# Float64 weights to float32 on the chip: shifts, masks and an integer addition in place of mantissa times exponent

## The chip, the cores and the metric

The kernel runs on one core of a Trainium2 chip. The time is that of one execution on the device, in microseconds (us). A core has five engines with their own in-order queues: TensorE (PE in the profile, PEld for its weight loads), VectorE (DVE), ScalarE (ACT), GpSimd (POOL) and SyncE (SP), which here issues all the transfers.

## The reference

Three stages, each on 8 batches of 576 positions and 512 features:

```python
kv = np.einsum('bhsd,bhse->bhde', k, v)            # attention without softmax
out = np.einsum('bhsd,bhde->bhse', q, kv)
x = out / np.sqrt(np.mean(out * out, -1, keepdims=True) + 1e-06) * g_norm

mixed = np.real(np.fft.fft(np.fft.fft(x, axis=1), axis=2))    # stage 2 (after heads are joined)
u = x + mixed
un = (u - mean(u)) / np.sqrt(var(u) + 1e-06)
x = u + np.maximum(un @ w_ch1, 0.0) @ w_ch2                   # 512 x 2048 and 2048 x 512

u = x + (x.transpose(0, 2, 1) @ U @ V).transpose(0, 2, 1)     # stage 3, U and V of rank 32
return u + np.maximum(u @ w_ch1, 0.0) @ w_ch2                 # its own w_ch1, w_ch2
```

The four weight matrices and U, V come as float64, because they are scaled by a float64 number; everything else is float32.

## The kernel before, in words

The positions (8 x 576 = 4608) are cut into 9 blocks of 512. Each of the two multilayer stages runs over the 9 blocks, and a block over 16 iterations, one per 128 of the 2048 hidden features: 12 matmuls for the hidden layer (`emit_l1`, L162), 12 for the output (`emit_l2`, L177). Every factor is split into a high part and a rest (`w1h`, `w1l`, `w2h`, `w2l`, `gh`, `gl`, `xh`, `xl`), so that each product is three matmuls. Iteration n, in the loop at L779, emits the split of the second weights (`split_w2`: ScalarE copies the high part, VectorE or, in iterations 5 to 9 of the first block, GpSimd subtracts), the hidden matmuls with `gh` on ScalarE and `gl` on VectorE, the split of the first weights two iterations ahead (`split_w1`, the subtraction on GpSimd or in some iterations on VectorE), then the output matmuls of the iteration before and a list of side tasks. The order on every engine is the order in which the program writes the instructions down (`manual_schedule`, L676); the lists `side` (L664) say which task stands in which iteration. During stage 2 the side tasks prepare the attention and the Fourier transform of the next batch: sums of squares (L267), powers (L269), norms (L280, L282), foldings (L295 to L330), transforms (L349 to L384).

The conversion. A weight tile is 128 x 512 float64 words. `raw_load` (L74) brings them, as pairs of 32-bit words, into one of two buffers `raw`; a load is issued for the tile two further on when a tile is converted (`w_next`, L119). `convert` (L99) takes a pair of tiles: `conv_a` for both, then `conv_b` for both. `lw` and `hw` are the low and the high words, 8 bytes apart. Per tile:

- L85, VectorE: the exponent bits of the high word into `pw`. L86, ScalarE: eight times that with the bias 896 taken off, as a number, which gives the bits of the float32 power of two. L87, ScalarE: the low word as a float, times 2^-52.
- L88, VectorE: the mantissa bits with the leading one, into the tile itself. L93, VectorE: the sign into `pw`. L95, VectorE: mantissa times 2^-20 plus the low part. L97, GpSimd: that times `pw`.

`pw` (tag `cv1`) has two buffers. Tiles of stage 2 are converted by `w_conv` (L115): one pair before the loop in two halves (L719 to L728), one pair each at L734 and L745, and 13 pairs in iterations 0 to 12 of block 0 (L766). Tiles of stage 3 are converted in stage 2 by `w_pre` (L124), which writes the result to DRAM, in iterations 0, 7 and 9 (`PRE`) of blocks 1 to 5 and once in block 6. Three more conversions (U and V) follow in block 7 (`t_b_tables`, L539). In all these places the conversion stands at the end of the iteration's side tasks.

Of the kernel before, what the change touches and what calls it, by code (L numbers as in the profile page):

```python
# [10 lines left out]
F32 = mybir.dt.float32  # L11
F32R = mybir.dt.float32r
U32 = mybir.dt.uint32
AF = mybir.ActivationFunctionType
ALU = mybir.AluOpType
# [17 lines left out]
VPAD = 192  # L33
EPS = 1e-6


@with_exitstack
def kernel(ctx: ExitStack, tc: tile.TileContext, qT, kvm, kvt, gn, w1a, w2a, w1b, w2b,
                      ucat, v4, tabs, outT):
    nc = tc.nc  # L40
    f32 = lambda ap: ap.bitcast(F32)

    com = ctx.enter_context(tc.tile_pool(name="com", bufs=1))
# [23 lines left out]
    ident = com.tile([128, 128], F32, name="ident")  # L67
    xe0 = com.tile([C, 3, B], F32, name="xe0")
    nhalf = com.tile([128, 8], F32, name="nhalf")
    ebias = com.tile([128, 1], F32, name="ebias")  # L70
    muT = com.tile([128, NT // 128], F32, name="muT")


# [5 lines left out]

    def conv_a(raw, out):  # L80

        n = raw.shape[1]
        lw, hw = raw[:, :, 0], raw[:, :, 1]
        pw = com.tile([128, 512], U32, tag="cv1", name="cv1", bufs=2)[:, 0:n]
        nc.vector.tensor_scalar(out=pw, in0=hw, scalar1=0x7FF00000, scalar2=None, op0=ALU.bitwise_and)  # L85
        nc.scalar.activation(out=pw, in_=pw, func=AF.Relu, scale=8.0, bias=ebias)  # L86
        nc.scalar.activation(out=f32(lw), in_=lw, func=AF.Copy, scale=2.0 ** -52)  # L87
        nc.vector.tensor_scalar(out=out.bitcast(U32), in0=hw, scalar1=0xFFFFF, scalar2=0x100000,  # L88
                                op0=ALU.bitwise_and, op1=ALU.bitwise_or)
        return raw, out, pw  # L90

    def conv_b(raw, out, pw):
        nc.vector.scalar_tensor_tensor(out=pw, in0=raw[:, :, 1], scalar=0x80000000, in1=pw,  # L93
                                       op0=ALU.bitwise_and, op1=ALU.bitwise_or)
        nc.vector.scalar_tensor_tensor(out=out, in0=out.bitcast(U32), scalar=2.0 ** -20, in1=f32(raw[:, :, 0]),  # L95
                                       op0=ALU.mult, op1=ALU.add)
        nc.gpsimd.tensor_tensor(out=out, in0=out, in1=f32(pw), op=ALU.mult)  # L97

    def convert(*pairs):  # L99
        for c in [conv_a(*p) for p in pairs]:  # L100
            conv_b(*c)
# [298 lines left out]
    def load_kv(b):  # L400
        kv = at.tile([128, 2, 5, DM], F32, tag="slot_a", name=f"kv{b}")
        for c in (slice(0, 256), slice(256, 512)) if b == 0 else (slice(0, 512),):
            for a in range(2):
                nc.sync.dma_start(out=kv[:, a, 0:4, c], in_=kvm[b][:, a, :, c])
            nc.sync.dma_start(out=kv[0:64, :, 4, c], in_=kvt[b][:, :, c])
        st.setdefault(b, {})["kv"] = kv
# [269 lines left out]
    with tc.manual_schedule():  # L676
        make_identity(nc, ident)
        nc.vector.memset(nhalf, -0.5)
        nc.vector.memset(kvbd, 0.0)
        nc.vector.memset(ebias, -896.0 * 2.0 ** 23)  # L680
        load_kv(0)
        load_q(0)
        nc.sync.dma_start(out=gnb, in_=gn)
# [33 lines left out]
        load_kv(1)  # L717
        t_s1(0, 0, 0)
        cv = [conv_a(raws.pop(0), w_new(0))]  # L719
        t_s1(0, 0, 1)  # L720
        t_s1(0, 1, 0)
        t_s1(0, 1, 1)
        conv_b(*cv[0])
        t_s2(0, 0)
        cv.append(conv_a(raws.pop(1), w_new(1)))
        t_ln_first(0)
        conv_b(*cv[1])
        w_next((0, 1))  # L728
        done = 2
# [158 lines left out]
```

## Time and profile before

| | |
|---|---|
| median of 3 runs | 1957.66 us (1957.63 to 1962.66) |
| the profiled execution | 1957.75 us, its span 1956.0 us |
| TensorE busy | 1849.6 us (95% of the span) |
| VectorE busy | 1000.8 us (51%) |
| ScalarE busy | 780.0 us (40%) |
| GpSimd busy | 769.8 us (39%) |
| granted TensorE clock, mean | 0.976 |

The span runs from the first to the last instruction of the profiled execution; its own time is 1.75 us longer. A busy time is the time in which an engine has an instruction running, also one that is running but held up. A duration in a row includes what the instruction waits once it has started; the step from one start to the next on the same engine is what it costs when the engine is full.

### The profile page before, as it was taken

The numbers are of one execution on the slowest core, as the hardware profiler recorded it, in microseconds if no ns is written. First come the engines' busy times: TensorE is split into PE (matmuls) and PEld (weight loads), VectorE is DVE, ScalarE is ACT, GpSimd is POOL, SyncE is SP. The second block draws the span as 40 slices with busy tenths as digits, with TensorE's granted clock in tenths as the row PEclk, the third lists the DMA queues.
The fourth block names the chain that finished last, engine by engine and source line by source line (L and its number), as shares of the span: only waits on it lengthen the run. The fifth ranks groups of instructions, "written<-read, shape, count | busy, mean of one in ns | idle before, by whom it ended". The sixth has DMA issues, their size and how long they took to land.

```text
span 1956.0 us, 22839 instructions
## 1 busy us (share of the span) xinstructions
PE 1849.6 (95%) x8520; PEld 1516.8 (78%) x8520; DVE 1000.8 (51%) x1525; ACT 780.0 (40%) x1460; POOL 769.8 (39%) x592
## 2 busy tenths in 40 slices
PE   4667899999899998999999999999999999999999
PEld 3556678878787887878888888888888888888887
DVE  5898785776757576574443333333333333333232
ACT  4444344444434444343434343434343433333332
POOL 4486665554545554453322223232223222222322
PEclk7878999999999999999999999999999999999999
DMA  4524415133241422302303301010101010100000
GB/s 137 192 86 150 174 44 193 68 119 130 73 146 54 163 98 97 133 10 74 87 33 131 122 1 49 1 44 1 49 0 44 1 49 1 44 1 22 1 22 22
DMA packets 62545, 140.05 MB, mean 72 GB/s; under 512 B 11273, under 2 KB 13786, under 8 KB 59618
## 3 DMA queue, kind: packets, MB, share of 16 engines
q1 hardware_dynamic: 62434, 138.59, 20.7%
q8 instruction: 67, 1.10, 0.2%
q14 instruction: 44, 0.36, 0.1%
HBM read 100.78 MB, written 36.73 MB: 70 GB/s over the span
## 4 chain that ended last, share of the span: by engine, by line
PE 75%; DVE 12%; POOL 6%; issue 3%; DMA 2%; ACT 2%; SPq 0%; DVEq 0%; POOLq 0%; ACTq 0%
PE h L168 11%; PE h L170 11%; PE h L169 11%; PE acc L193 7%; PE acc L194 7%; PE acc L192 7%; PE acc L188 4%; PE acc L190 4%; PE acc L189 4%; POOL ss L269 2%; PE kv L244 2%; POOL x L282 2%; DMA raw<-in_w2a 2%; DVE f L301 2%; DVE eh L330 1%
## 5 line engine op out<-in xcount | busy, mean ns | idle before, releaser
L146 POOL TENSOR_TENSOR w1l<-w,w1h 128x512 fp32r<-128x512 f32 x274 | 357.3, 1304 | 976.6 <-ACT w1h L145 953.3
L174 DVE SCALAR_TENSOR_TENSOR gl<-h,gh 128x512 fp32r<-128x512 f32 x288 | 198.3, 689 | 393.5 <-ACT gh L173 393.4
L173 ACT ACTIVATE gh<-h 128x512 fp32r<-128x512 f32 x288 | 171.4, 595 | 502.8 <-PE h L170 502.7
L154 DVE TENSOR_TENSOR w2l<-w,w2h 128x512 fp32r<-128x512 f32 x283 | 208.9, 738 | 188.4 <-ACT w2h L153 187.6
L188 PE MATMUL acc<-w2h,gl 128*128 128x512 f32 x576 | 235.4, 409 | 46.0 <-DVE gl L174 45.9
L153 ACT ACTIVATE w2h<-w 128x512 fp32r<-128x512 f32 x288 | 180.8, 628 | 160.7 <-PE acc L194 113.0
L189 PE MATMUL acc<-w2l,gh 128*128 128x512 f32 x576 | 232.0, 403 | 7.3 <-POOL w2l L154 7.3
L168 PE MATMUL h<-xl,w1h 128*128 128x512 f32 x576 | 230.0, 399 | 2.9 <-ACT w1h L145 1.4
L190 PE MATMUL acc<-w2h,gh 128*128 128x512 f32 x576 | 231.6, 402 | 0.0
L168 PE MATMUL h<-xlb,w1h 128*128 128x512 f32 x576 | 231.1, 401 | 0.0
L170 PE MATMUL h<-xhb,w1l 128*128 128x512 f32 x576 | 228.3, 396 | 0.0
L170 PE MATMUL h<-xh,w1l 128*128 128x512 f32 x576 | 226.2, 393 | 2.2 <-POOL w1l L146 2.2
L169 PE MATMUL h<-xhb,w1h 128*128 128x512 f32 x576 | 228.1, 396 | 0.0
L169 PE MATMUL h<-xh,w1h 128*128 128x512 f32 x576 | 226.2, 393 | 0.0
L194 PE MATMUL acc<-gh,w2h 128*128 128x512 f32 x576 | 225.4, 391 | 0.0
L193 PE MATMUL acc<-gl,w2h 128*128 128x512 f32 x576 | 225.4, 391 | 0.0
L192 PE MATMUL acc<-gh,w2l 128*128 128x512 f32 x576 | 224.7, 390 | 0.0
L145 ACT ACTIVATE w1h<-w 128x512 fp32r<-128x512 f32 x288 | 179.3, 623 | 23.2 <-POOL w L97 23.2
L188 PEld LDWEIGHTS acc<-w2h,gl 128*128 128x128 f32 x576 | 111.5, 194 | 79.2 <-DVE gl L174 56.0
L189 PEld LDWEIGHTS acc<-w2l,gh 128*128 128x128 f32 x576 | 112.2, 195 | 31.3 <-POOL w2l L154 8.7
L190 PEld LDWEIGHTS acc<-w2h,gh 128*128 128x128 f32 x576 | 112.5, 195 | 24.5
L170 PEld LDWEIGHTS h<-xh,w1l 128*128 128x128 f32 x576 | 109.3, 190 | 26.3 <-POOL w1l L146 2.6
(164 smaller groups left out, 2845.4 us busy)
## 6 DMA issues: line engine op xcount, KB each, us to landing
kv<-in_kvm SPq DMA_DIRECT2D x14, 1024.0 KB, 6.5
q<-in_qT SPq DMA_DIRECT2D x8, 1220.0 KB
x_d<-x2o SPq DMA_DIRECT2D x36, 256.0 KB, 2.1
x2f<-x_d SPq DMA_DIRECT2D x36, 256.0 KB, 3.8
outT<-o SPq DMA_DIRECT2D x36, 256.0 KB, 2.0
raw<-in_w1a SPq DMA_DIRECT2D x16, 512.0 KB, 3.4
raw<-in_w2a SPq DMA_DIRECT2D x16, 512.0 KB, 3.7
u_d<-x SPq DMA_DIRECT2D x32, 256.0 KB, 2.6
```

The costliest lines, as they stand in the source:

```text
L146: (nc.vector if n in on_dve else nc.gpsimd).tensor_tensor(out=al, in0=a, in1=f32(ah), op=ALU.subtract)
L154: (nc.gpsimd if n in CLP else nc.vector).tensor_tensor(out=cl, in0=c, in1=f32(ch), op=ALU.subtract)
L168: nc.tensor.matmul(out=h, lhsT=ah[:, kc, :], rhs=xl[:, kc, :], start=(kc == 0), stop=False)
L169: nc.tensor.matmul(out=h, lhsT=ah[:, kc, :], rhs=xh[:, kc, :], start=False, stop=False)
L170: nc.tensor.matmul(out=h, lhsT=al[:, kc, :], rhs=xh[:, kc, :], start=False, stop=(kc == 3))
L174: nc.vector.scalar_tensor_tensor(out=gl, in0=h, scalar=0.0, in1=f32(gh), op0=ALU.max, op1=ALU.subtract)
L188: nc.tensor.matmul(out=a, lhsT=gl[:, tt], rhs=ch, start=s, stop=False)
L189: nc.tensor.matmul(out=a, lhsT=gh[:, tt], rhs=cl, start=False, stop=False)
L190: nc.tensor.matmul(out=a, lhsT=gh[:, tt], rhs=ch, start=False, stop=e)
L192: nc.tensor.matmul(out=a, lhsT=cl[:, tt], rhs=gh, start=s, stop=False)
L193: nc.tensor.matmul(out=a, lhsT=ch[:, tt], rhs=gl, start=False, stop=False)
L194: nc.tensor.matmul(out=a, lhsT=ch[:, tt], rhs=gh, start=False, stop=e)
```

## The change

`ebias` and its memset go, and the conversion of a tile becomes: ScalarE takes the absolute value of the high word, read as a float32; VectorE clamps it between two constants (the patterns 0x38000000 and 0x47EFFFFF); ScalarE multiplies the low word by 2^-29 and stores it as an integer, which leaves its upper three bits, rounded; VectorE shifts the clamped word left by three and masks it. Then VectorE puts the top two bits of the high word and the rounded low part together in `pw`, and GpSimd adds the two as 32-bit integers. The places of the conversion, the buffers and the loads stay. Per tile VectorE has three instructions where it had four, ScalarE two as before, GpSimd one as before; the first instruction of a tile is now on ScalarE.

```diff
+HMIN, HMAX = (float(v) for v in np.array([0x38000000, 0x47EFFFFF], np.uint32).view(np.float32))
...
-    ebias = com.tile([128, 1], F32, name="ebias")
...
         lw, hw = raw[:, :, 0], raw[:, :, 1]
         pw = com.tile([128, 512], U32, tag="cv1", name="cv1", bufs=2)[:, 0:n]
-        nc.vector.tensor_scalar(out=pw, in0=hw, scalar1=0x7FF00000, scalar2=None, op0=ALU.bitwise_and)
-        nc.scalar.activation(out=pw, in_=pw, func=AF.Relu, scale=8.0, bias=ebias)
-        nc.scalar.activation(out=f32(lw), in_=lw, func=AF.Copy, scale=2.0 ** -52)
-        nc.vector.tensor_scalar(out=out.bitcast(U32), in0=hw, scalar1=0xFFFFF, scalar2=0x100000,
-                                op0=ALU.bitwise_and, op1=ALU.bitwise_or)
+        nc.scalar.activation(out=f32(pw), in_=f32(hw), func=AF.Abs)
+        nc.vector.tensor_scalar(out=f32(pw), in0=f32(pw), scalar1=HMIN, scalar2=HMAX, op0=ALU.max, op1=ALU.min)
+        nc.scalar.activation(out=lw, in_=lw, func=AF.Copy, scale=2.0 ** -29)
+        nc.vector.tensor_scalar(out=out.bitcast(U32), in0=pw, scalar1=3, scalar2=0x3FFFFFF8,
+                                op0=ALU.logical_shift_left, op1=ALU.bitwise_and)
         return raw, out, pw
 
     def conv_b(raw, out, pw):
-        nc.vector.scalar_tensor_tensor(out=pw, in0=raw[:, :, 1], scalar=0x80000000, in1=pw,
+        nc.vector.scalar_tensor_tensor(out=pw, in0=raw[:, :, 1], scalar=0xC0000000, in1=raw[:, :, 0],
                                        op0=ALU.bitwise_and, op1=ALU.bitwise_or)
-        nc.vector.scalar_tensor_tensor(out=out, in0=out.bitcast(U32), scalar=2.0 ** -20, in1=f32(raw[:, :, 0]),
-                                       op0=ALU.mult, op1=ALU.add)
-        nc.gpsimd.tensor_tensor(out=out, in0=out, in1=f32(pw), op=ALU.mult)
+        nc.gpsimd.tensor_tensor(out=out.bitcast(U32), in0=out.bitcast(U32), in1=pw, op=ALU.add)
...
-        nc.vector.memset(ebias, -896.0 * 2.0 ** 23)
```

## Rows read from the trace of the kernel before

**Rows 1.** The page, the chain that ended last, share by engine.

```profile
PE 75%; DVE 12%; POOL 6%; issue 3%; DMA 2%; ACT 2%; SPq 0%; DVEq 0%; POOLq 0%; ACTq 0%
```

**Rows 2.** Busy times by stage; the first row names the columns.

```profile
core 0: us, PE busy (x) PEld busy (x) DVE busy (x) ACT busy (x) POOL busy (x), PEclk, DMA share, GB/s
...
93.00:246.00 153.00, 119.94 (x505) 93.93 (x505) 126.20 (x188) 69.54 (x132) 105.35 (x69) 0.88 0.41 136
246.00:361.00 115.00, 110.89 (x548) 92.41 (x547) 78.58 (x123) 49.27 (x99) 58.96 (x46) 0.99 0.32 111
361.00:476.00 115.00, 110.91 (x549) 92.45 (x547) 78.74 (x123) 49.38 (x99) 59.13 (x46) 0.99 0.32 111
...
945.00:1956.00 1011.00, 1007.13 (x4460) 820.39 (x4458) 342.82 (x505) 375.68 (x651) 271.18 (x211) 1.00 0.10 34
```

**Rows 3.** Groups, 79 to 246 us: count, busy us, mean ns, idle before and releasers.

```profile
L97 POOL TENSOR_TENSOR w<-w,cv 128x512 f32<-128x512 f32 x28 | 45.9, 1648 | 36.8 <-DVE w L95 36.8
L95 DVE SCALAR_TENSOR_TENSOR w<-w,raw 128x512 f32<-128x512 uint32 x28 | 28.3, 1012 | 0.0
L93 DVE SCALAR_TENSOR_TENSOR cv<-raw,cv 128x512 uint32<-128x512 uint32 x28 | 20.5, 733 | 3.8 <-ACT cv L86 3.8
L86 ACT ACTIVATE cv<-cv,ebias 128x512 uint32<-128x512 uint32 x28 | 20.1, 718 | 30.0 <-DVE cv L85 30.0
L87 ACT ACTIVATE raw<-raw 128x512 f32<-128x512 uint32 x28 | 18.8, 670 | 0.0
L85 DVE TENSOR_SCALAR cv<-raw 128x512 uint32<-128x512 uint32 x28 | 16.6, 592 | 9.0 <-DMA raw<-in_w1a 5.9 <-DMA raw<-in_w2a 2.0 <-POOL w L97 1.2
```

**Rows 4.** VectorE in order of time, iteration 0 of block 2: start us, us, instruction.

```profile
364.54 0.42 DVE L88 TENSOR_SCALAR wpre<-raw 128x512 uint32<-128x512 uint32 x1
364.88 0.42 DVE L85 TENSOR_SCALAR cv<-raw 128x512 uint32<-128x512 uint32 x1
...
365.55 0.69 DVE L93 SCALAR_TENSOR_TENSOR cv<-raw,cv 128x512 uint32<-128x512 uint32 x1
366.17 0.68 DVE L95 SCALAR_TENSOR_TENSOR wpre<-wpre,raw 128x512 f32<-128x512 uint32 x1
...
367.37 1.76 DVE L95 SCALAR_TENSOR_TENSOR wpre<-wpre,raw 128x512 f32<-128x512 uint32 x1
369.06 0.68 DVE L154 TENSOR_TENSOR w2l<-w,w2h 128x512 fp32r<-128x512 f32 x1
...
370.26 1.20 DVE L146 TENSOR_TENSOR w1l<-w,w1h 128x512 fp32r<-128x512 f32 x1
371.38 1.28 DVE L280 TENSOR_TENSOR x<-x,ss 128x512 f32<-128x512 f32 x2
```

**Rows 5.** GpSimd in order of time, the same stretch.

```profile
367.10 1.49 POOL L97 TENSOR_TENSOR wpre<-wpre,cv 128x512 f32<-128x512 f32 x1
369.21 1.69 POOL L97 TENSOR_TENSOR wpre<-wpre,cv 128x512 f32<-128x512 f32 x1 [0.63 <-DVE wpre L95]
```

**Rows 6.** ScalarE in order of time, the same stretch.

```profile
362.64 0.62 ACT L265 ACTIVATE x<-o 128x512 f32<-128x512 f32 x1
364.66 0.73 ACT L86 ACTIVATE cv<-cv,ebias 128x512 uint32<-128x512 uint32 x1 [1.40 <-DVE cv L85]
365.29 0.67 ACT L87 ACTIVATE raw<-raw 128x512 f32<-128x512 uint32 x1
```

**Rows 7.** VectorE in order of time, start-up.

```profile
54.77 0.86 DVE L85 TENSOR_SCALAR cv<-raw 128x512 uint32<-128x512 uint32 x1
...
57.03 0.69 DVE L95 SCALAR_TENSOR_TENSOR w<-w,raw 128x512 f32<-128x512 uint32 x1
...
64.26 0.43 DVE L85 TENSOR_SCALAR cv<-raw 128x512 uint32<-128x512 uint32 x1 [1.06 <-DMA raw<-in_w2a]
...
66.74 1.75 DVE L95 SCALAR_TENSOR_TENSOR w<-w,raw 128x512 f32<-128x512 uint32 x1
```

**Rows 8.** Who waited for whom, whole span: us in total, times, longest us.

```profile
ACT cv L86 <- DVE cv L85: 65.8, 43, 5.4
...
DVE cv L93 <- ACT cv L86: 4.7, 4, 2.6
```

**Rows 9.** Line 97: count, least, median and greatest ns, first and last start us.

```profile
L97 POOL TENSOR_TENSOR w<-w,cv x32: 1260/1645/2868, 52.4 to 225.8; 128x512 f32<-128x512 f32 x32
```

**Rows 10.** Groups of ScalarE, whole span, columns as in Rows 3.

```profile
L248 ACT ACT_TABLE_LOAD x1 | 1.3, 1283 | 1.5 <-DVE ebias L680 1.5
```

## The prediction, made before the changed kernel was timed

> **What bounds the kernel now.** I read the chain that ended last first, then the busy times by stage, the costliest groups of the first block, and last the engines' order of time at one place of each kind. The chain is TensorE for 75% of the span, VectorE for 12% and GpSimd for 6% [rows 1]: a shorter conversion can only touch the last two. The stages say where they lie [rows 2]. Blocks 1 and 2 take 115 us each with TensorE busy 110.9 of them, and from 945 us on it is busy 1007 of 1011. Block 0 takes 153 us for the same matmuls, with VectorE busy 126 and GpSimd 105. Its difference to block 1 is the conversion: 13 pairs of weight tiles in block 0, three pairs (iterations 0, 7 and 9) in each of blocks 1 to 5, one in block 6. So there are three places to price: the start-up up to 79 us, the 14 pairs from 79 to 246 us, and the pair at iteration 0 of blocks 1 to 6. Iterations 7 and 9 of those blocks lie where the chain is TensorE, and the three late conversions of U and V come after 945 us, where TensorE fills the time; a shorter conversion there I cost at nothing, covered by the matmuls. Without that cover the ten pairs would be worth 12 us more at the price found below.
>
> What a tile costs on VectorE unhindered is read off the steps between starts: L85 and L88 0.34 us each, L93 and L95 some 0.60 us each [rows 4]. The second L95 of a pair takes 1.76 us, and in the same time GpSimd runs the first tile's product L97 [rows 4, 5]; the L146 on VectorE, held up by the second L97, takes 1.20. In the groups of the first block L95 has a mean of 1012 ns against 733 for L93 [rows 3]: about 1.1 us of waiting per pair on top of the work.
>
> **The change part by part.**
> - VectorE, removed: L85, L88, L93, L95, or 2 x 0.34 + 2 x 0.60 = 1.88 us a tile. Added: a clamp (one operand and two constants, packed words), shift and mask (the same shape), and one L93-like combination of two strided operands: 2 x 0.34 + 0.60 = 1.28 us. The clamp and the shift have no row of their own. L88 is nearest, two operations with constants at the same price as L85; the upper bound is 0.60, a two-operand pass, which is 0.26 us a tile for each, and a packed source could save up to 0.1. I take 0.34. Net: 0.60 us a tile, 1.2 us a pair.
> - The wait inside L95. Taken from that row alone, a pair saves 1.2 + 1.1 = 2.3 us. But the L146 row shows that another VectorE operation with two SBUF operands is held just the same when GpSimd runs. After the change the first addition starts when the second combination ends, and the next such operation, mostly w2l (L154), meets it. So the 1.1 us is not saved, it moves, and 1.2 us remains; 2.3 is kept as the other bound. The Trainium skill, "SBUF — State Buffer", section "SBUF: two separate sides", says the same as a rule: VectorE, in a two-port mode or with two SBUF inputs, and GpSimd take one port pair as an exclusive lock for a whole instruction. By that rule it is 1.2 a pair, by the row of L95 alone 2.3.
> - ScalarE: Relu with a bias becomes Abs, and the copy of the low word only gets another scale and type: 0.72 and 0.67 before, the same after, bounds 0.6 to 0.75 [rows 3, 6]. If Abs wanted another function table, each switch would cost a load as in the one row there is, 1.28 us [rows 10], two per tile; no row shows Abs. The Trainium skill, "ScalarE: Activation LUTs", section "Table sets: the hidden batching unit", lists abs among the functions that every set holds; by that it is nothing.
> - The order between the engines. Before, VectorE began on the words themselves and ScalarE waited for L85: 65.8 us in 43 cases, against 4.7 us in 4 cases the other way [rows 8]. After, Abs goes first and VectorE waits for it. Queued behind that wait on VectorE are the combination, w2l, gl, and behind gl TensorE. Mostly the new wait is covered, since ScalarE stood idle ahead of L86: at 363.26 us it is free (362.64 plus 0.62), at 364.66 it starts [rows 6]; Abs would run 1.4 us sooner and the second Abs ends near 365.05, where VectorE wants it at 364.9: 0.2 us of waiting. Where ScalarE itself is late (VectorE's L93 waits 3.8 us for it from 79 to 246 us [rows 3], 4 times in the whole span [rows 8]), the pair now starts with VectorE idle: Abs to the end of the second combination takes 3.1 us, where four old operations took 2.4 plus the 1.1 that moves. Three of the 14 pairs I count so, at no gain, bounds -0.7 and +0.4 each.
> - GpSimd: a float product becomes a sum of 32-bit integers. No row has an integer operation there. The nearest are the product (least 1260, median 1645 ns with its waits, [rows 9]) and, for word type, VectorE's L93 on integers, no slower than L95 with a float among its operands. I take 1.27 us, no change. Lower bound 1.1; for the upper bound I take twice, 2.54.
> - Transfers: a raw buffer is freed by the one combination instead of by L95, 0.6 us sooner for a first and up to 1.7 us for a second tile. VectorE waits for raw words 7.9 us in all from 79 to 246 us [rows 3], so this is part of the same 1.2 us and not a second gain; the Abs now stands between landing and clamp (0.7 us), which uses up most of it.
> - The removed memset of ebias runs while the first loads are under way: nothing.
>
> **The sum.** Start-up: the single tile at 54.77 ends its L95 at 57.72 [rows 7], 2.9 us. After: Abs and the low word are long done (ScalarE idle), 1.28 us, gain 1.5 with its margins. The pair whose second tile lands at 64.26 ends at 68.49 [rows 7], 4.2 us; after: Abs 0.7, clamp, shift 0.68, two combinations 1.2, or 2.6, gain 1.6; what follows there reads PSUM or one operand, so nothing is held up instead. Together 3.1. From 79 to 246 us: 11 pairs x 1.2 and three at nothing, 13.2. Blocks 1 to 6, iteration 0: the chain runs through the pair, w2l, w1l and x [rows 4]; 1.2 less the 0.2 of waiting and 0.1 for a changed meeting with GpSimd, 0.9 x 6 = 5.4. Sum 21.7 us. The profiled execution took 1957.75 us (span 1956.0 and 1.75 around it), 0.09 above the median of the runs, so the same sum holds for both: **1936 us**.
>
> **The rivals.**
> 1. The port wait does not move but goes: the additions fall beside operations on PSUM, and raw words arrive early enough. 2.3 a pair: 14 x 2.3 + 3.5 + 6 x 2 = 48, or 1910 us. For it: in iterations 5 to 9 w2l is on GpSimd, and VectorE's next operation, gl, reads PSUM. Against: L146 and w2l are there in most of the others.
> 2. ScalarE sets the pace: a shorter VectorE catches up with it, and half of the pairs begin with a wait. Then 7 x 1.2 - 7 x 0.7 = 3.5, start-up 1.5, blocks nothing: 1953 us. For it: 20.1 and 18.8 us of ScalarE on the conversion of this stretch alone [rows 3]. Against: the 30 us in which it waited for L85 there.
> 3. Slower: the integer sum is slow on GpSimd. Place: L97, ahead of w1h in block 0 and of the norm's products at the block starts. With twice the duration, 1.27 more on 40 additions (28 and 12) is 51 us if all of it lies on the path, half if half does: 51 or 25 less 22 gives between 1961 and 1987, middle 1974. It decides from about +0.5 us an addition (21.7 / 40). For it: GpSimd is busy 105 of 153 us in block 0, so a longer operation has little cover. Against: sum, difference and product of floats have one duration there.
> 4. The change does not do what it says on the engine's side: Abs brings table loads. Some 134 of 1.28 us, a third of them on the path, about 1990 us.
>
> **How the numbers follow.** Forecast 0.64 (its own range 1924 to 1946), rival 1 0.13, rival 2 0.09, rival 3 0.12, rival 4 0.02. The range leaves out rivals 3 and 4 and a little of rival 1: 1908 to 1953, which takes in the 2.3 bound and the slow bound of clamp and shift (14 x 2 x 0.26 is 7 us). A measurement of this kernel tells about 0.3%, 6 us, from no change. Faster: forecast and rival 1 with a remnant of the rest, 0.78; same: rival 2, 0.08; slower: rivals 3 and 4, 0.14.
>
> **What would show it.** Right: VectorE has three instructions a tile at about 0.42, 0.42 and 0.68 us; the addition's least duration stays at 1.26 to 1.29 us; w2l (L154) or another two-operand operation after a pair grows to 1.7 us where L95 did; block 0 is 10 to 15 us shorter than 153 us, blocks 1 to 6 about 1 us each, and nothing changes from 945 us on. A gap ahead of the second clamp, released by Abs, is some 0.2 us, not over 1 us on most pairs. Wrong: an addition over 1.8 us, a second table load, or VectorE idle for Abs by more than 10 us in block 0; in the other direction, w2l staying at 0.7 us after the pairs.

## The result, and the profile after

The median of the changed kernel is **1942.99 us** (1940.88 to 1945.39, 4 runs), beside 1959.74 us (1957.63 to 1962.66) for the kernel before on the same chip: ratio 0.9916, 95% interval 0.9900 to 0.9932. That is 16.7 us less (13.3 to 19.6 by the interval) where 21.7 were forecast: the direction was right and the time lies within the range, but the gain is clearly smaller than forecast. The profiled execution took 1943.31 us (span 1941.6), 14.4 less than the profiled execution of before.

The page of the changed kernel, busy times and the chain that ended last:

```profile
PE 1844.0 (95%) x8520; PEld 1514.0 (78%) x8520; DVE 965.5 (50%) x1457; ACT 773.8 (40%) x1460; POOL 752.9 (39%) x592
...
PE 83%; DVE 8%; ACT 3%; DMA 2%; POOL 2%; issue 1%; SPq 0%; DVEq 0%; ACTq 0%; POOLq 0%
```

Against [rows 1] VectorE's part of the chain falls from 12 to 8% and GpSimd's from 6 to 2; TensorE takes their place. VectorE is busy for 35 us less, more than twice what the time gained. The busy times by stage, after:

```profile
core 0: us, PE busy (x) PEld busy (x) DVE busy (x) ACT busy (x) POOL busy (x), PEclk, DMA share, GB/s
93.00:233.00 140.00, 113.14 (x503) 90.21 (x502) 110.01 (x159) 65.31 (x127) 93.82 (x68) 0.90 0.41 144
233.00:348.00 115.00, 110.56 (x556) 92.26 (x555) 77.28 (x119) 49.65 (x101) 58.74 (x47) 1.00 0.32 111
...
945.00:1941.00 996.00, 992.69 (x4396) 808.57 (x4394) 334.40 (x493) 368.69 (x638) 266.11 (x208) 1.00 0.10 33
```

The first block is 13 us shorter than the 153 of [rows 2]. The stages that follow look alike in this view, so I cut each profile at two marks that can be read in the order of time: the start of the first `gl`, and, as the end of each block, the start of the third of its four additions `x2o`. "Late" and "early" count the stretches in which the granted clock falls to half in blocks 1 to 6, behind the pause of iteration 7 or of iteration 5; they are explained with run e3_clock.

| kernel | first `gl` | block 0 | blocks 1 to 6 | late | early |
|---|---|---|---|---|---|
| before | 84.74 | 161.59 | 685.72 | 1 | 4 |
| after | 83.32 | 150.03 | 684.37 | 4 | 0 |
| e1_pad | 87.93 | 165.78 | 690.76 | 3 | 3 |
| e2_noabs | 81.58 | 142.96 | 684.22 | 4 | 0 |
| e3_clock | 85.59 | 150.00 | 678.23 | 0 | 0 |
| e4_stage2 | 81.23 | 151.44 | 688.83 | 3 | 3 |
| e5_add2 | 87.21 | 169.82 | 691.10 | 0 | 6 |
| e6_early | 86.01 | 164.04 | 684.08 | 4 | 0 |
| e7_inter | 85.46 | 151.50 | 682.83 | 4 | 0 |
| e8_all | 82.00 | 163.58 | 676.99 | 0 | 0 |
| e9_pick | 85.27 | 144.38 | 684.46 | 4 | 0 |
| e10_pick_clock | 81.95 | 146.52 | 678.68 | 0 | 0 |
| e11_noabs_clock | 81.14 | 142.27 | 678.02 | 0 | 0 |
| e12_oldfill5 | 86.34 | 162.37 | 691.59 | 5 | 0 |

Each row is one execution. Where the code up to the end of block 0 is the same, block 0 takes 150.0, 150.0 and 151.4 us (after, e3_clock, e4_stage2), 144.4 and 146.5 (e9_pick, e10_pick_clock), 143.0 and 142.3 (e2_noabs, e11_noabs_clock), 161.6 and 162.4 (before, e12_oldfill5); a difference of 2 us there shows nothing of an edit.

The rest, from the end of block 6 to the end of the span, is 1023.8 to 1024.4 us in all of them but one (e3_clock, 1027.0). So the 14.4 us are 1.4 up to the first `gl`, 11.6 in block 0, 1.4 in blocks 1 to 6 and nothing behind: the forecast had 3.1, 13.2 (with one pair ahead of the first `gl`), 5.4 and nothing. The first and the last of the three terms came out at less than half.

The groups of the changed kernel from 79 to 233 us, as [rows 3] has them for before:

```profile
L98 POOL TENSOR_TENSOR w<-w,cv 128x512 uint32<-128x512 uint32 x28 | 44.1, 1596 | 35.3 <-DVE cv L96 35.3
L96 DVE SCALAR_TENSOR_TENSOR cv<-raw 128x512 uint32<-128x512 uint32 x28 | 18.9, 715 | 0.0
L90 ACT ACTIVATE raw<-raw 128x512 uint32<-128x512 uint32 x27 | 18.2, 674 | 0.0
L88 ACT ACTIVATE cv<-raw 128x512 f32<-128x512 f32 x27 | 18.1, 670 | 6.2 <-DMA raw<-in_w1a 5.9
L155 DVE TENSOR_TENSOR w2l<-w,w2h 128x512 fp32r<-128x512 f32 x12 | 16.9, 1406 | 0.0
L89 DVE TENSOR_SCALAR cv<-cv 128x512 f32<-128x512 f32 x28 | 16.6, 594 | 15.2 <-ACT cv L88 15.2
L91 DVE TENSOR_SCALAR w<-cv 128x512 uint32<-128x512 uint32 x28 | 15.1, 540 | 1.0
```

Three things are to be read here. The combination L96 has a mean of 715 ns, no longer the 1012 of L95: it is not held up. `w2l` (L155, which was L154) has 1406 ns, twice the 0.68 us that one takes unhindered, where the kernel before had 808: the wait sits there now. And the clamp L89 stands behind 15.2 us of idle VectorE, released by Abs (L88), where L85 had 9.0 for all its reasons and L93 another 3.8. The row of `w2l` in the kernel before, from 79 to 246 us:

```profile
L154 DVE TENSOR_TENSOR w2l<-w,w2h 128x512 fp32r<-128x512 f32 x12 | 9.7, 808 | 0.0
```

VectorE and, in the second fence, GpSimd of the changed kernel in order of time at iteration 0 of block 2, which answers to [rows 4, 5]:

```profile
350.12 0.42 DVE L89 TENSOR_SCALAR cv<-cv 128x512 f32<-128x512 f32 x1
350.57 0.43 DVE L91 TENSOR_SCALAR wpre<-cv 128x512 uint32<-128x512 uint32 x1
350.92 0.42 DVE L89 TENSOR_SCALAR cv<-cv 128x512 f32<-128x512 f32 x1
351.44 0.43 DVE L91 TENSOR_SCALAR wpre<-cv 128x512 uint32<-128x512 uint32 x1
351.79 1.29 DVE L96 SCALAR_TENSOR_TENSOR cv<-raw 128x512 uint32<-128x512 uint32 x2
352.99 1.76 DVE L155 TENSOR_TENSOR w2l<-w,w2h 128x512 fp32r<-128x512 f32 x1
354.68 0.68 DVE L175 SCALAR_TENSOR_TENSOR gl<-h,gh 128x512 fp32r<-128x512 f32 x1
355.28 1.18 DVE L147 TENSOR_TENSOR w1l<-w,w1h 128x512 fp32r<-128x512 f32 x1
```

```profile
352.80 3.10 POOL L98 TENSOR_TENSOR wpre<-wpre,cv 128x512 uint32<-128x512 uint32 x2
```

The two additions run from 352.80 to 355.90, and the 1.76 of `w2l` and the 1.18 of `w1l` lie inside, as 1.76 of L95 and 1.20 of L146 lay beside the products before. The step from clamp to shift is 0.45 and 0.52 us, not 0.34: the shift reads what the clamp has just written, while the step from the shift to the next, independent clamp is 0.35.

Passes with one operand take longer beside GpSimd too: L89 and L91 have means of 594 and 540 ns above, where one alone takes some 430. In iteration 3 of block 0 a shift took 1.41 us and the clamp behind it 1.51, while GpSimd ran two multiplications L283:

```profile
112.34 1.41 DVE L91 TENSOR_SCALAR w<-cv 128x512 uint32<-128x512 uint32 x1
113.67 1.51 DVE L89 TENSOR_SCALAR cv<-cv 128x512 f32<-128x512 f32 x1
```

```profile
111.91 2.99 POOL L283 TENSOR_TENSOR x<-x,gnb 128x512 f32<-128x512 f32 x2
```

### The profile page after: what moved, and what is told of

Same layout as the page of the kernel before. It is cut to its first block, busy times and chain, and to the rows that moved or that the text cites. A ratio compares the mean times of both kernels' runs of the same rounds, so it can differ in the third digit from the quotient of the medians.

```text
span 1941.6 us, 22765 instructions
## 1 busy us (share of the span) xinstructions
PE 1844.0 (95%) x8520; PEld 1514.0 (78%) x8520; DVE 965.5 (50%) x1457; ACT 773.8 (40%) x1460; POOL 752.9 (39%) x592
## 4 chain that ended last, share of the span: by engine, by line
PE 83%; DVE 8%; ACT 3%; DMA 2%; POOL 2%; issue 1%; SPq 0%; DVEq 0%; ACTq 0%; POOLq 0%
PE h L169 12%; PE h L171 12%; PE h L170 12%; PE acc L194 7%; PE acc L195 7%; PE acc L193 7%; PE acc L189 6%; PE acc L191 6%; PE acc L190 6%; PE kv L245 2%; DVE f L302 2%; DVE eh L331 1%; PE o L263 1%; DMA raw<-in_w1a 1%; PE pt L599 1%
## 5 line engine op out<-in xcount | busy, mean ns | idle before, releaser
L155 DVE TENSOR_TENSOR w2l<-w,w2h 128x512 fp32r<-128x512 f32 x283 | 230.6, 815 | 189.6 <-ACT w2h L154 188.8
L154 ACT ACTIVATE w2h<-w 128x512 fp32r<-128x512 f32 x288 | 181.2, 629 | 160.5 <-PE acc L195 113.0
L146 ACT ACTIVATE w1h<-w 128x512 fp32r<-128x512 f32 x288 | 179.8, 624 | 33.9 <-POOL w L98 33.9
L169 PEld LDWEIGHTS h<-xlb,w1h 128*128 128x128 f32 x576 | 108.3, 188 | 26.7 <-issue 2.5
```

Of the source, the lines that this page charges most:

```text
L155: (nc.gpsimd if n in CLP else nc.vector).tensor_tensor(out=cl, in0=c, in1=f32(ch), op=ALU.subtract)
L169: nc.tensor.matmul(out=h, lhsT=ah[:, kc, :], rhs=xl[:, kc, :], start=(kc == 0), stop=False)
```

## The experiments

All are edits of the changed kernel but e12_oldfill5, which is one of the kernel before. The diffs show the lines that matter; helper code is left out at `...`. Lines in the fences are those of each run's own kernel.

**e1_pad: a fourth pass on VectorE.** It gives VectorE as many passes a tile as before and leaves the new order alone.

```diff
         nc.vector.scalar_tensor_tensor(out=pw, in0=raw[:, :, 1], scalar=0xC0000000, in1=raw[:, :, 0],
                                        op0=ALU.bitwise_and, op1=ALU.bitwise_or)
+        nc.vector.scalar_tensor_tensor(out=pw, in0=pw, scalar=0xFFFFFFFF, in1=pw,
+                                       op0=ALU.bitwise_and, op1=ALU.bitwise_or)
```

> The changed kernel with one more VectorE pass per tile, placed between the combination and GpSimd's addition: pw = (pw and all ones) or pw, which changes nothing in the values and does not read the raw words. VectorE has four instructions a tile again (0.34 + 0.34 + 0.60 + 0.60 us); the raw buffers are freed as early as in the changed kernel, and Abs still goes first. Theory (VectorE's time between the pairs and what follows is what was gained): the gain is given back, 1955 to 1962 us, ratio to the kernel before 0.998 to 1.002, block 0 back to some 153 us. Rival (the gain comes from raw buffers that are freed sooner, or from ScalarE going first): it stays at 1943 us, ratio 0.990 to 0.993.

Measured: 1968.54 us, ratio to before 1.0032 (1.0020 to 1.0045). The whole gain is gone, and more: the time lies above the 1955 to 1962 of the theory. Block 0 is 15.75 us longer than in the changed kernel: over its 13 pairs 1.21 us each, the price of the forecast. Groups of VectorE in e1_pad, whole span:

```profile
L157 DVE TENSOR_TENSOR w2l<-w,w2h 128x512 fp32r<-128x512 f32 x283 | 212.6, 751 | 187.2 <-ACT w2h L156 186.6
L98 DVE SCALAR_TENSOR_TENSOR cv<-cv 128x512 uint32<-128x512 uint32 x64 | 73.5, 1149 | 2.2
```

With the extra pass the wait is back in the conversion (1149 ns) and `w2l` has 751, as in the kernel before (738); without it `w2l` has a mean of 815 over the span. So in these kernels the wait falls on the two-operand pass of VectorE that meets GpSimd's addition. The same run prices the new order, with the shift that depends on its clamp: with four passes each, block 0 is 165.8 us with Abs first and 161.6 in the kernel before. The raw buffers, which it frees as early as the changed kernel does, do not keep the gain; a part of their own, hidden by the cost of the order, is not ruled out.

**e2_noabs: no Abs, VectorE first.** The clamp reads the high word itself, from -HMAX to HMAX; the lower clamp at HMIN is left out.

```diff
-        nc.scalar.activation(out=f32(pw), in_=f32(hw), func=AF.Abs)
-        nc.vector.tensor_scalar(out=f32(pw), in0=f32(pw), scalar1=HMIN, scalar2=HMAX, op0=ALU.max, op1=ALU.min)
+        nc.vector.tensor_scalar(out=f32(pw), in0=f32(hw), scalar1=-HMAX, scalar2=HMAX, op0=ALU.max, op1=ALU.min)
```

> The changed kernel without Abs: VectorE clamps the high word itself between plus and minus the upper bound (one pass, 8-byte stride), the sign bit falls out in the shift and mask. Left out: the lower clamp, which catches values under float32's smallest exponent. VectorE keeps three passes a tile, ScalarE has one pass where it had two, and the first instruction of a tile is VectorE's again. VectorE waited 20.4 us for Abs in 25 cases in the changed kernel, some of it behind transfers that it waits for anyway. Theory (that wait lies partly on the path from 54 to 246 us): 3 to 8 us under the changed kernel, 1935 to 1940 us, ratio 0.987 to 0.990. Rival (the wait stands for landings and is hidden): 1943 us, ratio 0.990 to 0.993. If the strided clamp should be slow, VectorE's first pass shows over 0.43 us.

Measured: 1936.93 us, ratio 0.9873 (0.9860 to 0.9886). Block 0 is 7.1 us shorter than with Abs; blocks 1 to 6 are the same (684.2). What Abs costs, it costs in block 0. The edit also takes ScalarE's pass of 0.67 us out of each tile, so the 7.1 us are the price of Abs as a whole, the waiting and the pass; the run does not part the two. There the clamp's own row becomes, from 79 to 225 us:

```profile
L88 DVE TENSOR_SCALAR cv<-raw 128x512 f32<-128x512 f32 x26 | 14.7, 565 | 5.2 <-DMA raw<-in_w1a 4.8 <-DMA raw<-in_w2a 0.3
```

**e3_clock: matmuls that nobody reads.** In the changed kernel, TensorE in order of time in iteration 7 of block 2:

```profile
388.43 0.39 PE L171 MATMUL h<-xh,w1l 128*128 128x512 f32 x1
391.07 0.50 PE L189 MATMUL acc<-w2h,gl 128*128 128x512 f32 x1 [2.25 <-DVE gl L175]
...
392.33 0.56 PE L191 MATMUL acc<-w2h,gh 128*128 128x512 f32 x1
392.69 0.63 PE L189 MATMUL acc<-w2h,gl 128*128 128x512 f32 x1
393.12 0.63 PE L190 MATMUL acc<-w2l,gh 128*128 128x512 f32 x1
```

After a pause of 2.25 us the steps between matmuls go from 0.23 to 0.43 us until 395.25. The stretches of 15 us around that pause, in blocks 2 and 3:

```profile
388.00:403.00 15.00, 12.75 (x53) 9.98 (x52) 9.04 (x17) 10.14 (x22) 3.23 (x3) 0.89 0.45 158
503.00:518.00 15.00, 12.77 (x60) 10.09 (x59) 10.02 (x17) 10.72 (x23) 4.22 (x4) 1.00 0.46 159
```

The column of the granted clock has 0.89 and 1.00: the same pause, half clock (1.2 GHz) behind it in block 2 and not in block 3. Block 2 takes 115.66 us, block 3 114.03. The run fills the pauses:

```diff
+            if i in (5, 7) and 1 <= j <= 7:
+                xh = xt[j][0]
+                dm = ps_s.tile([128, 512], F32, tag="side", name=f"dm{n}")
+                for _ in range(9 if i == 7 else 5):
+                    nc.tensor.matmul(out=dm, lhsT=xh[:, 0, 0:128], rhs=xh[:, 0, :], start=True, stop=True)
             if i > 0:
                 emit_l2(n - 1)
```

> The changed kernel with 5 more matmuls (128x512, no reader) in iteration 5 and 9 in iteration 7 of blocks 1 to 7, just ahead of the output matmuls that wait for gl, so that TensorE has work in the two pauses of 0.8 and 2.25 us ahead of them. Theory (blocks 2, 4, 5 and 6 of the changed kernel lose 1.55 us each to a stretch at half the granted clock that follows the pause): the rows at half speed after the pause are gone, all of blocks 1 to 5 take 114 to 114.6 us, in all 3 to 6 us under the changed kernel, 1937 to 1940 us, if the added matmuls fit into the pauses. Rival (the loss is from another wait, or the clock falls all the same): two or more blocks of 115.6 us remain; 1943 to 1948 us, since the added matmuls cost up to 0.5 us a block and about 3 us in block 7, where there is no pause.

Measured: 1940.80 us, ratio 0.9892 (0.9876 to 0.9908), just above the 1940 of the theory. Blocks 1 to 6 take 678.2 us, 6.1 less than in the changed kernel, and every one of blocks 1 to 5 between 114.00 and 114.20: no stretch at half clock is left. In block 7, where TensorE has no pause to fill, the 14 matmuls cost 3.1 us (the rest of the span is 1027.0 instead of 1023.9), which is why the whole time shows so little. TensorE in iteration 7 of block 2 of this run:

```profile
391.06 2.20 PE L796 MATMUL dm<-xh 128*128 128x512 f32 x9
393.47 0.50 PE L189 MATMUL acc<-w2h,gl 128*128 128x512 f32 x1 [0.21 <-DVE gl L175]
```

The stretch around it, busy times with the granted clock at 1.00:

```profile
390.00:405.00 15.00, 14.79 (x70) 11.80 (x68) 10.19 (x17) 10.54 (x23) 4.39 (x4) 1.00 0.44 158
```

**e4_stage2: the new conversion for the tiles of stage 2 (and U, V) alone.** `w_pre` keeps the old one as `convert0`, `ebias` returns.

```diff
-        convert(*((raws.pop(s), w) for s, w in zip(ss, ws)))
+        convert0(*((raws.pop(s), w) for s, w in zip(ss, ws)))
```

> The new conversion only for the weights of stage 2 (start-up and block 0) and for U and V; the weights of stage 3, converted in blocks 1 to 6, by the old one. Theory (13 us of the gain lie before 246 us, and blocks 1 to 6 gain 1.0 us each but lose most of it to stretches at half clock): block 0 and the start-up as in the changed kernel, blocks 1 to 6 at 115.0 us each with no more than two at 116.6, in all 1943 to 1947 us, ratio 0.991 to 0.994. Rival (the conversions in blocks 1 to 6 carry a good part of the gain): 1949 us or more, ratio over 0.995.

Measured: 1945.82 us, ratio 0.9919 (0.9906 to 0.9933). Blocks without a late stretch take 115.0 us as before, against 114.0 with the change: 1.0 us a block is what the new conversion brings there, near the 0.9 of the forecast. By the time of all runs little of it is left: the ratio of the changed kernel is 0.9916, 0.6 us better, within the noise. The profile also says how far the late stretches can vary: blocks 1 to 6 are here those of the kernel before, with the same pauses, and have three late ones where that has one.

**e5_add2: a second addition on GpSimd.** It stands behind the first and writes to `pw`, which nobody reads afterwards.

```diff
         nc.gpsimd.tensor_tensor(out=out.bitcast(U32), in0=out.bitcast(U32), in1=pw, op=ALU.add)
+        nc.gpsimd.tensor_tensor(out=pw, in0=out.bitcast(U32), in1=pw, op=ALU.add)
```

> The changed kernel with a second integer addition per tile on GpSimd, right behind the first (its sum goes into pw, which nobody reads afterwards): what a slow addition would have cost. It adds 1.26 us and more on 64 weight tiles, 32 of them before 246 us and 12 at the block starts. Theory of the prediction (half of it lies on the path): 25 us more than the changed kernel, 1960 to 1975 us, ratio 0.999 to 1.008. All of it on the path: 1985 us or more. Rival (GpSimd has room, so the speed of the addition hardly matters): under 1952 us.

Measured: 1973.02 us, ratio 1.0061 (1.0045 to 1.0076), 30 us over the changed kernel. Block 0 grows by 19.8, 0.76 an addition over 26 of them. Blocks 1 to 5 take 116.2 us instead of the 114.0 of one without a late stretch, 1.1 for each of the two additions of iteration 0; together blocks 1 to 6 grow by only 6.7, as the stretches at half clock lie early in this run. So the third rival's place and price were right. The rival did not come about because an integer addition takes what a product took, 1255 ns at least where [rows 9] has 1260. Line 98 of the changed kernel:

```profile
L98 POOL TENSOR_TENSOR w<-w,cv x32: 1255/1654/1752, 51.7 to 212.7; 128x512 uint32<-128x512 uint32 x32
```

**e6_early: both Abs of a pair at the front of the iteration's side tasks.**

```diff
...
+    def w_abs(*ss):
+        for s in ss:
+            w = ahead[s] = w_new(s)
+            nc.scalar.activation(out=w, in_=f32(raws[s][:, :, 1]), func=AF.Abs)
...
-            side[k * CONV[4] * 2 // (2 * NF - done)].append(lambda m=m: w_conv(m, m + 1))
+            at_n = k * CONV[4] * 2 // (2 * NF - done)
+            side[at_n].insert(0, lambda m=m: w_abs(m, m + 1))
+            side[at_n].append(lambda m=m: w_conv(m, m + 1))
```

> The changed kernel with the two Abs of a pair in block 0 moved from the end of the iteration's side tasks to their front, written into the weight tile instead of pw; all else at its place. Theory (Abs came late in the pairs of iterations 4 to 6, behind ScalarE's copies that wait for GpSimd and for foldings, and that cost 1.5 to 1.9 us each): VectorE's waits for Abs from 93 us on shrink to under 3 us, 3 to 7 us under the changed kernel, 1936 to 1940 us, ratio 0.987 to 0.990. Rival (an Abs at the front waits for its words to land and holds up the copies behind it, what is won there is lost): 1942 us or more.

Measured: 1958.08 us, ratio 0.9984 (0.9975 to 0.9994): a miss. My theory of the run falls (1936 to 1940 us), the rival holds (1942 or more). Block 0 is 14 us longer. The Abs at the front, from 79 to 250 us:

```profile
L120 ACT ACTIVATE w<-raw 128x512 f32<-128x512 f32 x26 | 17.4, 669 | 31.5 <-DMA raw<-in_w1a 20.5 <-DMA raw<-in_w2a 11.0
```

ScalarE now waits 31.5 us for raw words that have not landed, with the splits and squares of the iteration queued behind. From one `gl` to the next, iterations 3 to 7 are 0.3 to 1.5 us shorter each, where the words are there, and 1, 2, 8 and 10 to 12 are 1.6 to 6.4 longer.

**e7_inter: the two tiles interleaved, so that no shift follows its own clamp.**

```diff
     def convert(*pairs):
-        for c in [conv_a(*p) for p in pairs]:
-            conv_b(*c)
+        cs = [conv_a(*p) for p in pairs]
+        for f in (conv_m, conv_s, conv_b):
+            for c in cs:
+                f(*c)
...
```

Here `conv_a` holds what ScalarE does, `conv_m` the clamp and `conv_s` the shift.

> The changed kernel with the work of a pair interleaved: both Abs, then both copies of the low words on ScalarE, both clamps, then both shifts on VectorE. Theory (a shift that reads what the clamp just ahead of it wrote starts 0.46 us after it instead of 0.34, and the second Abs stood behind the first copy): 0.24 us a pair and up to 0.5 us where VectorE waits for the second Abs, 3 to 6 us in all under the changed kernel, 1937 to 1941 us, ratio 0.9875 to 0.990; the step from one clamp to the next is 0.34 us. Rival (these gaps are filled by GpSimd, which holds the next two-operand pass instead): 1942 us or more.

Measured: 1941.14 us, ratio 0.9909 (0.9895 to 0.9923). Not told apart by the time. Blocks without a late stretch take 113.8 us instead of 114.0, about the two dependent steps of a pair; block 0 is 1.5 longer, hardly more than the 1.4 of e4_stage2, whose code in block 0 is that of the changed kernel.

**e8_all: e6, e7 and the matmuls of e3 (in blocks 1 to 6) together.**

> Abs at the front in block 0, the interleaved pair, and the matmuls without a reader in the pauses of blocks 1 to 6 (not in block 7) together; nothing of the computation is left out. If the three parts are independent: 5 + 4 + 6 us under the changed kernel, 1926 to 1933 us, ratio 0.982 to 0.986, blocks 1 to 5 at 113.5 to 114.2 us each. Rival (early Abs and interleaving win the same waits): 1931 to 1936 us.

Measured: 1949.68 us, ratio 0.9944 (0.9932 to 0.9957): a miss, far above both the theory and the rival (1926 to 1936). Blocks 1 to 6 are the shortest of all, 677.0 us, but block 0 has the 13.5 us of e6_early. What e6 lost is not mended by the interleaving.

**e9_pick: Abs at the front in iterations 3 to 6 only.** The diff is against e6_early.

```diff
-            side[at_n].insert(0, lambda m=m: w_abs(m, m + 1))
+            if 3 <= at_n <= 6:
+                side[at_n].insert(0, lambda m=m: w_abs(m, m + 1))
```

> The changed kernel with one thing of the run that moved every Abs of block 0 to the front of its iteration: here only the pairs of iterations 3, 4, 5 and 6 have their two Abs moved (written into the weight tile), the other pairs keep the order of the change. Nothing is left out. Theory (the Abs-first order costs where ScalarE is late, and moving it pays only where the raw words have landed by the start of the iteration): in the run with all pairs moved the steps from one gl to the next shrank by 1.1 to 1.5 us in these iterations and grew in 1, 2, 8, 10, 11 and 12; so 4 x 1.3 = about 5 us less than the changed kernel, some 1938 us, ratio to the kernel before 0.987 to 0.990. Rival (the loads follow the conversion, so an earlier conversion in four iterations only makes the next ones wait longer for their raw words): within 1.5 us of the changed kernel, 0.990 to 0.993.

Measured: 1940.44 us, ratio 0.9900 (0.9885 to 0.9915), between the two by the time. The order of time decides: the steps from one `gl` to the next in iterations 4, 5 and 6 are 1.5, 1.35 and 1.3 us shorter than after, here and in e10_pick_clock, and iteration 3 gains nothing: 4.1 us. Block 0 as a whole is 5.7 shorter here and 3.5 in e10_pick_clock, with the same code; the first `gl` came 2 us later in this execution, for a reason that is none of the edit (below). Why it gains is seen in iteration 4 of the changed kernel, ScalarE in order of time:

```profile
124.69 0.63 ACT L285 ACTIVATE x<-x 34x512 f32<-34x512 f32 x1 [2.48 <-POOL x L283]
125.34 0.66 ACT L88 ACTIVATE cv<-raw 128x512 f32<-128x512 f32 x1
```

And VectorE in the same place:

```profile
126.11 0.43 DVE L89 TENSOR_SCALAR cv<-cv 128x512 f32<-128x512 f32 x1 [2.82 <-ACT cv L88]
```

Abs could go (its loads left SyncE's queue at 116.31 and 116.87, and the median from issue to landing is 3.9 and 4.4 us), but it stands in ScalarE's queue behind L285, which waits 2.48 us for GpSimd's `x`; VectorE stands idle for 2.82. In e9_pick Abs runs at 121.28 and 123.48, ahead of what L285 is there, and VectorE has no gap ahead of its clamp (L90 in that kernel):

```profile
123.39 1.77 DVE L288 TENSOR_TENSOR x<-x,ss 98x512 f32<-98x512 f32 x1
125.08 0.41 DVE L90 TENSOR_SCALAR w<-w 128x512 f32<-128x512 f32 x1
```

**e10_pick_clock: e9 and the matmuls of e3 in blocks 1 to 6.** Nothing is left out, and this is the fastest kernel here that computes all of it.

> The kernel of the run with four moved pairs, and in iterations 5 and 7 of blocks 1 to 6 the 5 and 9 matmuls that nobody reads, ahead of the second layer of the iteration before. Nothing is left out. Theory (two costs that add up: the order in block 0, and the stretches at half clock in blocks 2, 4, 5 and 6): 4 x 1.55 less 6 x 0.2 for the added matmuls, about 5 us less than the run with four moved pairs, 1932 to 1935 us, ratio 0.984 to 0.9875. Rival (what block 0 gains is lost again to the clock or to the loads): 1938 to 1941, ratio 0.989 to 0.991, as the run with the matmuls alone.

Measured: 1934.01 us, ratio 0.9865 (0.9847 to 0.9883), as the theory had it: 6.4 us less than e9_pick. The two costs add up, and this version beats both kernels.

**e11_noabs_clock: e2 and the same matmuls.**

> The run without Abs (the clamp is taken from -HMAX to HMAX on the high word itself; the lower clamp at HMIN is left out) with the same 5 and 9 matmuls that nobody reads in iterations 5 and 7 of blocks 1 to 6. Theory (Abs-first order and clock are separate costs): the run without Abs gave 1936.9 with four stretches at half clock; without these 4 x 1.55 less 6 x 0.2 = 5 us less, about 1932 us, ratio 0.9835 to 0.987. Rival (the blocks without Abs are bound by something else than TensorE): within 1.5 us of the run without Abs, 0.986 to 0.989.

Measured: 1930.63 us, ratio 0.9848 (0.9832 to 0.9864), as the theory had it: 6.3 us less than e2_noabs.

**e12_oldfill5: the kernel before, its pause in iteration 5 filled.** In the kernel before, the clock's rows show five stretches at half clock in blocks 1 to 6, and only the one in block 3, behind iteration 7, made its block longer (116.58 us; the other blocks from 1 to 5 take 115.0 to 115.1, with such a stretch or without). TensorE of the kernel before in block 3:

```profile
521.07 0.50 PE L188 MATMUL acc<-w2h,gl 128*128 128x512 f32 x1 [2.25 <-DVE gl L174]
...
522.47 0.63 PE L190 MATMUL acc<-w2h,gh 128*128 128x512 f32 x1
```

In block 2 TensorE of the kernel before shows where the free ones lie:

```profile
391.53 0.50 PE L188 MATMUL acc<-w2h,gl 128*128 128x512 f32 x1 [2.35 <-DVE gl L174]
...
392.64 0.63 PE L189 MATMUL acc<-w2l,gh 128*128 128x512 f32 x1
...
406.05 0.50 PE L188 MATMUL acc<-w2h,gl 128*128 128x512 f32 x1 [1.75 <-DVE gl L174]
```

The pause of 2.35 us is that of iteration 5. What the slow matmuls behind it lose comes out of the pauses that follow: the 0.8 us in iteration 6 is gone, and iteration 7 has 1.75 instead of 2.25. In the changed kernel the pauses are 1.44, 0.77 and 2.25, and the half clock comes behind the last, where no pause follows that could pay for it.

```diff
+            if i == 5 and 1 <= j <= 6:
+                xh = xt[j][0]
+                dm = ps_s.tile([128, 512], F32, tag="side", name=f"dm{n}")
+                for _ in range(5):
+                    nc.tensor.matmul(out=dm, lhsT=xh[:, 0, 0:128], rhs=xh[:, 0, :], start=True, stop=True)
```

> The kernel before, with 5 matmuls that nobody reads in iteration 5 of blocks 1 to 6, ahead of the second layer of the iteration before; nothing is left out. In the kernel before TensorE pauses 2.35 us in iteration 5 and 1.75 or 2.25 in iteration 7; the granted clock falls to half behind the pause of iteration 5 in four of six blocks (free: the pauses that follow are shorter by as much) and behind that of iteration 7 in one (1.55 us longer). Theory (a stretch at half clock costs nothing in iteration 5 and 1.55 us in iteration 7, and a kernel that no longer has the first gets the second): with the pause of iteration 5 cut to some 1.2 us the early stretches go, and iteration 7 gets them, in 3 to 5 blocks instead of one: blocks 1 to 6 together 688.8 to 692 us instead of 685.7, the time 3 to 6 us more, 1961 to 1966 us, ratio 1.001 to 1.0035. Rival (the two places are independent, and where the clock falls has nothing to do with the pause ahead): blocks 1 to 6 stay at 685.7 plus at most 6 x 0.2, the time within 1.2 us of the kernel before, ratio 0.9995 to 1.0007.

Measured: 1963.03 us, ratio 1.0008 (0.9998 to 1.0018): by the time alone between the two. The profiled execution follows the theory: no early stretch is left, five late ones have come, blocks 1 to 6 take 691.6 us, and blocks 1 to 4, which have one each, 116.5. But it is one profile, and with the pause of iteration 5 unfilled there were one late stretch in the kernel before and three in e4_stage2. In block 2 of e12_oldfill5:

```profile
395.35 0.50 PE L188 MATMUL acc<-w2h,gl 128*128 128x512 f32 x1 [1.21 <-DVE gl L174]
...
409.89 0.50 PE L188 MATMUL acc<-w2h,gl 128*128 128x512 f32 x1 [2.23 <-DVE gl L174]
...
411.05 0.63 PE L189 MATMUL acc<-w2l,gh 128*128 128x512 f32 x1
```

## Why the prediction was right, and which terms were off

**Right: the price of a pair.** "2 x 0.34 + 0.60 = 1.28 us" a tile and 1.2 us a pair stand; e1_pad takes 1.21 a pair away again. A part was off inside it: the shift behind its own clamp costs some 0.1 us more than a pass behind an independent one, 0.2 a pair, which the working did not have. The packed source saved nothing: clamp and shift take 0.42 and 0.43 us, as L88 does.

**Right: the wait moves.** "So the 1.1 us is not saved, it moves": `w2l` has 1.76 us behind a pair, two L96 take 1.29 together, and e1_pad moves the wait back. It is also not bound to two operands: one-operand passes are held beside GpSimd as well (L91 at 112.34 and L89 at 113.67 us), which the working did not have. The exclusive lock of the Trainium skill ("SBUF — State Buffer", section "SBUF: two separate sides") agrees with these rows. Rival 1, 2.3 us a pair, falls with it: even e2_noabs and the filled pauses together reach 1930.6, not 1910.

**Right: the addition and the function table.** The addition has the product's duration, and e5_add2 shows that the third rival would have cost what it was priced at: 30 us for one more addition a tile, between the 25 and the 51 us that the prediction works with. The single table load stayed single, as the Trainium skill ("ScalarE: Activation LUTs", section "Table sets: the hidden batching unit") had it for abs; in the groups of the changed kernel's ScalarE:

```profile
L249 ACT ACT_TABLE_LOAD x1 | 1.3, 1283 | 1.5 <-DVE kvbd L680 1.5
```

**Mis-sized: the start-up, 3.1 forecast, 1.35 measured.** First loads and first matmuls stood alike in the two profiled executions (the first Fourier matmul at 41.33 and 41.26 us), so 84.74 less 83.32, less 0.07, is the gain. The pair of 64.26 brought its 1.6: VectorE ended it at 66.90 instead of 68.49. The single tile of 54.77 ended 1.2 us sooner, but nothing came of that: the loads of the next pair left SyncE's queue at 56.72 instead of 57.11, behind three transfers of `un` that take 2.13 there, and the second tile was on ScalarE at 64.12, where VectorE had it at 64.26. The step that failed was to count both as path; the second waits for a landing that the first does not set. The pair after that, at 78 us, gained nothing: 0.38 of waiting for Abs and a `w2l` of 1.78.

**Mis-sized: the order in block 0.** "Three of the 14 pairs I count so, at no gain" is a loss of 3.6 us to the order. From 79 us to the end of block 0 the gain was 11.4 us, where 14 pairs x 1.2 are 16.8: the order and what else the working lacks cost 5.4. The place was right (a pair for which ScalarE is late), the number of pairs too small: VectorE waited 25 times for Abs in the span, 20.4 us in all; who waited for whom, in us, times and the longest:

```profile
DVE cv L89 <- ACT cv L88: 20.4, 25, 3.3
```

Without Abs block 0 would be 7.1 us less (e2_noabs). Not parted from this is the granted clock in block 0, 0.88 before and 0.90 after: both kernels have stretches at half clock there, and no run prices them. The prediction named "VectorE idle for Abs by more than 10 us in block 0" as a sign against it: at 15.2 us the sign was there. It cost less than feared because VectorE had stood idle 12.8 us ahead of L85 and L93 before, mostly for raw words and for L86 [rows 3].

**Failed: blocks 1 to 6, 5.4 forecast, 1.35 measured.** The step itself, 0.9 x 6, is right where it can be seen undisturbed: 115.0 to 114.0 in five blocks, 108.97 to 107.94 in the sixth (e3_clock), 6.0 in all. What the sum left out is the granted clock of TensorE, which falls to half behind some of its pauses, and the change moves the pauses. The change took the pause of iteration 5 from 2.35 to 1.44 us; the half clock that had followed there for free came behind iteration 7, at some 1.55 us a time, in four blocks instead of one: 3 x 1.55 = 4.7 of 6.0 given back. That filling the pauses brings it back is shown (e3_clock, e10_pick_clock, e11_noabs_clock): 6.1 us of blocks 1 to 6 in the profile of the first, more than 6 us in the time of the other two. That a shorter first pause moves the stretch to the second is what the profiles have in common: four late ones in each of the five kernels with a first pause of 1.1 to 1.5 us (after, e2_noabs, e6_early, e7_inter, e9_pick), five in e12_oldfill5; one in the kernel before and three in e4_stage2, which has the same code there. So the number varies from one execution of the same code to another. Against the blocks of e4_stage2 the gain is 4.5 us, and that it is only 1.35 in the profiled pair is in part luck; by the times it is 0.6 us between e4_stage2 and the changed kernel. Why the stretch falls in four blocks and not in the other two, behind pauses of 2.23 to 2.25 us in all six, stays open.

**Between the profile and the median.** The profiled pair differs by 14.4 us, the medians by 16.7. Executions of code that is the same up to the first `gl` reach it between 81.2 and 85.6 us (after, e3_clock, e4_stage2, e9_pick, e10_pick_clock): the first 40 matmuls, fed by the first loads, take 7.7 to 10.9 us. A start-up gain of 1 or 2 us can be read only with that difference taken off.

## What to carry to other kernels

Shortening VectorE's work by some passes saved the passes, not the wait beside GpSimd: that went to the next pass that met GpSimd's work. When the first instruction of a chain moves to another engine, look at what stands ahead of it in that engine's queue, and move it only as far forward as its data have landed. And where a shorter chain leaves TensorE with fewer or other pauses, read the granted clock behind each of them: here a stretch at half clock cost nothing where later pauses took it up, and 1.55 us where none did.

## What was not expected of the hardware

The place of a half-clock stretch decides its price: 0 us behind the pause of iteration 5 (block 2 of the kernel before 115.00 us with it, block 5 115.01 without), 1.55 us behind that of iteration 7 (116.58). Matmuls that nobody reads, nine of them (2.2 us of TensorE) in one pause and five in another, cost the block nothing: block 3 takes 114.05 us with them (e3_clock) and 114.03 without (the changed kernel, where the clock held). And a VectorE pass that reads what the one just before it wrote starts 0.45 us after it, where an independent one starts after 0.34 to 0.35.
